# A state-space scan and a gated feed-forward net on one core: the first chunk taken as two pairs of units by time, and the first four f tiles as half products

## The chip, the cores and the metric
The kernel runs on one core of one Trainium2 chip. A core has a matrix engine (TensorE, PE in the profile), VectorE (DVE), ScalarE (ACT), GpSimd (POOL), and SyncE (SP), on whose queue all DMAs of this kernel are issued. The metric is the device time of one execution in microseconds; the time before is the median of 3 runs.

## The reference
First a scan in chunks over four batches, eight heads, 768 tokens, 32 values and 16 states per head; then a gated feed-forward net over 3072 tokens of 256 values, with 1536 inner values:

```python
for c in range(nc):                       # chunks of 32 tokens
    cum = np.cumsum(la, axis=-1)          # la = log(clip(a))
    L = np.exp(cum[:, :, :, None] - cum[:, :, None, :]) * causal
    CB = np.einsum('bhin,bhjn->bhij', Cc, Bc)
    y_intra = np.einsum('bhij,bhjd->bhid', CB * L, xc)
    y_inter = np.einsum('bhin,bhnd->bhid', Cc, state) * decay_to_i[:, :, :, None]
    y[:, :, sl] = y_intra + y_inter
    state = decay_full[:, :, None, None] * state + np.sum(Bx, axis=2)
...
x = attn_out.transpose(0, 2, 1, 3).reshape(B * S, H * D)
gate = 1.0 / (1.0 + np.exp(-(x @ w_gate)))
return (gate * (x @ w_val)) @ w_out
```

## The kernel before, in words
The kernel takes 128 tokens as a chunk (`L`), in two halves of 64 (`L2`), so there are six chunks. A **unit** is one batch of one chunk: u = 4c + b, written c_b. For a unit, `products` transposes B and C on TensorE (tile `pt`), ScalarE copies them out (`bct`), and `multiply` makes the products of C and B (tile `pcb`); `decays` scans the decay factors on VectorE (`ab`), and `weigh` multiplies the two (`m`). `within` makes the outputs within each half and the local states, with 64 tokens on the partitions: 32 by 64 outputs, two at a time for the two halves of the chunk. What the state adds comes after. From chunk 1 on, two units are finished together (`results`). The output of the scan for 512 tokens (128 of each batch) is the moving operand of the net, `xw` in float32 for chunk 0, and a pair of rounded parts, `xh` and `xl`, for the others.

The net goes over twelve f tiles of 128 inner values: a gate product `pg` and a value product `pv` each, a sigmoid on ScalarE, a product of the two on VectorE (`h`), and four projections per chunk (`po`). A weight is loaded once (`wr`, 0.5 MB; w0 to w11 for gates (even) and values (odd), two f tiles each; w12 to w17 for the projection), put together by `split_w` over VectorE, ScalarE, VectorE, ScalarE and GpSimd, and later split by `part_w` into two rounded parts. In chunk 0 the f tiles 0 to 5 (`thin`) use whole weights and `xw`: two products of 128 by 512 each. The others use six products each (line 770). Products of the net go through three PSUM banks, `mm`.

In the first chunk (class `FirstUnit`) each of the four units is one batch with both halves, done one after another. `result` makes the two halves in two PSUM tiles, `py` and `mm`; the local state of the first half is spread by a mask to a 128 by 256 tile `wide` (line 614), and two products with full 128 by 128 stationary tiles (line 620) add what that state gives the second half. f tile 0 starts with 256 tokens of the first two batches (line 750), before the other two are done.

The order on every engine is written out ahead by a planner: tasks have a due time (`DUES` where given, else one worked out from constants such as `P0`, `CONV`, `UNIT1`), and `run` repeatedly takes the task that its own cost model lets start first, among those near each other the one that is due first. So all queues are in order, and an instruction that waits holds all behind it on its engine. The DMAs use eight semaphores in turn; the ninth waits for the first. The decays of chunk 1 and later come by way of DRAM: `a` is loaded (`r`), clipped, stored as `a_z` and its running products as `a_p`, and `ab` and `pp` are loaded from these.

Of the kernel before, what the change touches and what calls it, by code (L numbers as in the profile page):

```python
# [36 lines left out]
FIRST = "b0 x0 b1 x1 b2 x2 w0 b3 x3 w1 w2 w3 r w4 w5 w6 w7 w8 w9"  # L37
# [13 lines left out]
P0 = 35.5  # L51
UNIT0 = 4.5
CONV_D = 6.3
CONV = -30.0
UNIT1 = 52.0
UNIT1_D = 7.0
FFN1 = 77.0
# [11 lines left out]
def tile_ssd_then_gated_ffn(  # L69
# [28 lines left out]
    NPLAIN = 6  # L98
    NWHOLE = 12
# [21 lines left out]
    warm_sb = hp.tile([P, P], F32, tag="h6", name="warm_sb")  # L121
# [18 lines left out]
    eye2 = hp.tile([P, L2], F32, tag="h7", name="eye2")  # L140
# [16 lines left out]
    of_row = hp.tile([NB * H, P], F32, tag="h4", name="of_row")  # L157
# [170 lines left out]
    def part_w(i):  # L328
# [3 lines left out]
        if n > 1 and plain[order[n - 2]]:  # L332
            needs.append(("used", order[n - 2]) if order[n - 2] < NF else ("proj", 0))
# [26 lines left out]
    class Unit:  # L360
# [7 lines left out]
        def products(self):  # L368

            c, b, u = self.c, self.b, self.u  # L370
            needs = [("bc", u)]
            if c:
                needs += [("bct", u - 1 if c > 1 else -1), ("cb", u - 4), ("cd", u - 4)]
            needs += [("x", 0, NB - 1)] if c == 1 else []
            pool, tag, hold = (ps_y, "py", "y") if c else (ps_mm, "mm", "banks")
            yield step("pe", 0.24 if c else 0.45, needs, [("tp", u)], **{hold: 1})
            bn, cn = (got[k, c, b // 2][:, b % 2].rearrange("p h n -> p (h n)") for k in ("bn", "cn"))
            pt = pool.tile([P, 512], F32, tag=tag, name=f"pt{self.nm}")
            nc.tensor.transpose(pt[:, :L], bn, eye)
            nc.tensor.transpose(pt[:, L : 2 * L], cn, eye)  # L380
            yield step("act", 0.9 if c else 1.1, [], [("bct", u)], **{hold: -1})
            if c:
                self.bct = wk.tile([P, 4, L], F32, tag="bct", name=f"bct{self.nm}", bufs=4)
            else:

                if ("bct", b // 2) not in got:
                    got["bct", b // 2] = hp.tile([P, 2, 4, L], F32, tag=f"h{b // 2}", name=f"bct{self.nm}")
                self.bct = got["bct", b // 2][:, b % 2]
            if c:
# [5 lines left out]
            if c == 0:  # L395
                nc.scalar.copy(self.bct[:, 1, L2:], pt[:, L + L2 : 2 * L])
            units[u] = self
            if c == 0:
                yield step("pe", 0.47, [], [("cb", u)])
                if "pcb" not in got:  # L400
                    got["pcb"] = ps_cb.tile([P, NQ, 512], F32, tag="pcb", name="pcb0")
                multiply(got["pcb"], b, self)
# [17 lines left out]
        def decayed(self):  # L420
            c, b, u = self.c, self.b, self.u
            eng = yield step(("dve", "pool"), (0.28, 0.42), [("bc", u), ("scan", u), ("y", u - 4)], [("bdec", u)], port=True)
# [40 lines left out]
    def multiply_after(*us):  # L463

        then = [u + 2 for u in us]
        yield step("pe", 0.8, [("bct", u) for u in then], [("cb", u) for u in then], cb=1)
# [97 lines left out]
    class FirstUnit(Unit):  # L564


        def spread(self):

            b, u = self.b, self.u
            yield step("pe", 1.0, [("a0",)], banks=1)  # L570
            pa = ps_mm.tile([P, 512], F32, tag="mm", name=f"pa{b}")
            for i in range(2):
                rows = slice(32 * i, 32 * i + 32)
# [11 lines left out]
        def before(self):  # L585

            u, b = self.u, self.b
            eng = yield step(("dve", "pool"), (0.2, 0.3), [("bct", u), ("p0",)], [("cd", u)], port=True)
            self.cd = wk.tile([P, L], F32, tag="cd", name=f"cd{self.nm}", bufs=4)
            engines[eng].tensor_tensor(out=self.cd[:, L2:], in0=self.bct[:, 1, L2:], in1=got["p0"][:, b], op=ALU.mult)  # L590

        def last(self, i):
            return got["p0"][:, self.b, L2 - 1 : L2]
# [4 lines left out]
        def result(self):  # L598
            u, b = self.u, self.b
            yield step("dve", 0.68, [("cb", u), ("scan", u)], [("mult", u)])  # L600
            weigh(self)
            yield step("pe", 0.75, [("xn", u), ("first", u - 1), ("bdec", u)], [("y", u)], banks=1, y=1)
            self.py = py = [
                pool.tile([P, NK + 1, L2], F32, tag=tag, name=f"{tag}{self.nm}") for pool, tag in ((ps_y, "py"), (ps_mm, "mm"))
            ]
            within(
                self, lambda i, kt, rows: py[i][rows, kt], lambda i, rows: py[i][rows, NK], lambda kt: kt == 0
            )
            yield step("dve", 0.42, [("inter", u - 2)], [("wide", u)])
            if b == 0:  # L610
                got["wide"] = hp.tile([P, NB, NQ, NG, D], F32, tag="h3", name="wide")
            wide = got["wide"][:, b]
            local = py[0][:, NK].rearrange("p (o g d) -> p o g d", o=1, g=NG)
            nc.vector.tensor_tensor(
                out=wide, in0=local.broadcast_to([P, NQ, NG, D]),
                in1=of_h.rearrange("p (q g o) -> p q g o", g=NG, o=1).broadcast_to([P, NQ, NG, D]), op=ALU.mult,
            )
            yield step("pe", 0.42, [("cd", u)], [("inter", u)])
            for kt in range(NK):
                nc.tensor.matmul(  # L620
                    py[1][:, kt], wide[:, 2 * kt : 2 * kt + 2].rearrange("p q g d -> p (q g d)"), self.cd[:, L2:],
# [388 lines left out]
```

## Time and profile before

| | |
|---|---|
| median of 3 runs | 377.67 us (376.72 to 379.18) |
| profiled execution | 376.6 us, span 374.8 us |
| TensorE busy | 364.8 us, 97% of the span |
| VectorE, ScalarE, GpSimd busy | 155.2, 151.2, 156.2 us |
| granted TensorE clock | 1.00 to 17.5 us, 0.50 to about 31 us, 1.00 to the end |
| DMA | 26.27 MB, mean 70 GB/s; in the first 60 us 100 to 390 GB/s |

An engine's busy time counts instructions, not whether the end waits for them; here TensorE's queue is nearly gapless after the first 30 us, so a change shows in the end only where it changes the length of TensorE's queue, its gaps, or its clock. In the chain and in the timelines the first column is the start from the beginning of the span and the second the duration, in us. A wait stands in brackets: the idle time ahead of the instruction, and what ended it.

### The profile page before, as it was taken

What the parts mean: (1) busy time and instruction counts of PE and PEld (TensorE: products, weight loads), DVE (VectorE), ACT (ScalarE), POOL (GpSimd) and SP (SyncE); (2) the same over time, 40 slices, a digit from 0 to 9 for tenths busy, and PEclk for the clock granted to TensorE, in tenths of its full rate; (3) what the DMA queues carried; (4) which work ended last, traced back from release to release, by engine and by line L of the source; (5) the groups of instructions that cost most, each with busy time, mean ns of one, the idle gap of its engine ahead of it and who ended that gap; (6) DMA issues with size and microseconds to landing.
All of it is one profiled execution on the core that took longest, in us unless ns stands there. A gap on an engine that the chain in (4) does not pass through costs nothing.

```text
span 374.8 us, 8050 instructions
## 1 busy us (share of the span) xinstructions
PE 364.8 (97%) x3336; PEld 285.5 (76%) x3336; DVE 155.2 (41%) x280; ACT 151.2 (40%) x319; POOL 156.2 (42%) x161
## 2 busy tenths in 40 slices
PE   8779999999899999999999999999999999999996
PEld 2356468878688888888788888788877788888885
DVE  4765576863764234253431452450142440222201
ACT  2556677333546421446511435420335420244400
POOL 4454848764768540245430155430145420145410
PEclk9958999999999999999999999999999999999999
DMA  7999975187610052414402304120000000000000
GB/s 153 137 339 168 232 246 170 33 128 144 124 31 16 0 96 63 75 39 58 83 17 58 100 0 47 27 40 28 28 3 2 2 2 28 28 2 0 0 30 28
DMA packets 89270, 26.27 MB, mean 70 GB/s; under 512 B 76306, under 2 KB 82002, under 8 KB 89234
## 3 DMA queue, kind: packets, MB, share of 16 engines
q1 hardware_dynamic: 89234, 25.76, 31.2%
q8 instruction: 26, 0.43, 0.5%
q14 instruction: 10, 0.08, 0.1%
HBM read 22.41 MB, written 3.34 MB: 69 GB/s over the span
## 4 chain that ended last, share of the span: by engine, by line
PE 90%; SPq 4%; DMA 3%; DVE 1%; issue 0%; ACT 0%; DVEq 0%
PE pg L770 25%; PE pv L770 24%; PE po L807 15%; PE po L808 7%; PE po L796 5%; PE pv L761 2%; PE pg L761 2%; PE pcb L485 2%; SPq L261 2%; PE pcb L459 2%; DMA wr<-in_moe_w_val_dram 2%; PE pcb L536 1%; SPq L268 1%; PE pcb L492 1%; SPq L295 1%; DMA ab<-a_z 1%
## 5 line engine op out<-in xcount | busy, mean ns | idle before, releaser
L731 POOL TENSOR_TENSOR h<-g,h 128x512 fp32r<-128x512 f32 x60 | 78.9, 1315 | 124.1 <-ACT h L729 121.4
L770 PE MATMUL pg<-xh,w 128*128 128x512 f32 x264 | 93.8, 396 | 0.0
L770 PE MATMUL pv<-xh,w 128*128 128x512 f32 x264 | 93.7, 396 | 0.0
L807 PE MATMUL po<-w,h 128*128 128x512 f32 x228 | 81.9, 402 | 0.0
L725 DVE TENSOR_TENSOR g<-pv,g 128x512 f32<-128x512 f32 x60 | 41.5, 691 | 91.8 <-PE pv L770 86.9
L729 ACT CAST h<-g 128x512 fp32r<-128x512 f32 x60 | 37.3, 621 | 78.4 <-DVE g L725 78.4
L808 PE MATMUL po<-w,h 128*128 128x256 f32 x228 | 63.9, 280 | 0.0
L770 PEld LDWEIGHTS pg<-xh,w 128*128 128x128 f32 x264 | 49.5, 188 | 11.4 <-issue 0.7
L770 PEld LDWEIGHTS pv<-xh,w 128*128 128x128 f32 x264 | 49.6, 188 | 10.6 <-issue 0.2
L701 ACT ACTIVATE g<-pg 128x512 f32<-128x512 f32 x72 | 43.0, 597 | 22.6 <-PE pg L770 16.4
L770 PE MATMUL pg<-xl,w 128*128 128x512 f32 x132 | 51.5, 390 | 0.0
L770 PE MATMUL pv<-xl,w 128*128 128x512 f32 x132 | 51.4, 390 | 0.0
L807 PEld LDWEIGHTS po<-w,h 128*128 128x128 f32 x228 | 42.8, 188 | 10.7 <-issue 0.2
L808 PEld LDWEIGHTS po<-w,h 128*128 128x128 f32 x228 | 43.1, 189 | 0.2
L823 ACT COPY o<-po 128x256 f32<-128x256 f32 x20 | 7.5, 373 | 67.3 <-PE po L808 66.7
L825 DVE TENSOR_TENSOR o<-po,o 128x256 f32<-128x256 f32 x20 | 8.5, 424 | 59.8 <-ACT o L823 59.8
L339 POOL TENSOR_TENSOR w<-wr,w 128x512 fp32r<-128x512 f32 x18 | 24.4, 1359 | 12.3 <-ACT w L337 9.9
L770 PEld LDWEIGHTS pv<-xl,w 128*128 128x128 f32 x132 | 24.8, 188 | 4.7
L414 DVE TENSOR_TENSOR_SCAN ab<-ab,delta 128x512 f32<-128x512 f32 x20 | 25.7, 1286 | 6.5 <-DMA ab<-a_z 6.5
L770 PEld LDWEIGHTS pg<-xl,w 128*128 128x128 f32 x132 | 24.8, 188 | 4.6
L322 POOL TENSOR_TENSOR wr<-wr 128x512 int32<-128x512 int32 x18 | 21.6, 1206 | 9.0 <-ACT wr L320 4.5
L796 PE MATMUL po<-wr,h 128*128 128x256 f32 x96 | 23.6, 393 | 0.0
(104 smaller groups left out, 380.2 us busy)
## 6 DMA issues: line engine op xcount, KB each, us to landing
ab<-a_z SPq DMA_DIRECT2D x40, 128.0 KB
wr<-in_moe_w_gate_dram SPq DMA_DIRECT2D x6, 512.0 KB
wr<-in_moe_w_val_dram SPq DMA_DIRECT2D x6, 512.0 KB
wr<-in_moe_w_out_dram SPq DMA_DIRECT2D x6, 512.0 KB
out_dram<-o SPq DMA_DIRECT2D x24, 128.0 KB
xn<-in_x_dram SPq DMA_DIRECT2D x10, 256.0 KB
bn<-in_B_dram SPq DMA_DIRECT2D x10, 128.0 KB
cn<-in_C_dram SPq DMA_DIRECT2D x10, 128.0 KB
```

What stands on the lines that cost most here:

```text
L322: nc.gpsimd.tensor_tensor(out=lw.bitcast(I32), in0=hw.bitcast(I32), in1=lw.bitcast(I32), op=ALU.add)
L339: engines[eng].tensor_tensor(out=lo, in0=lw, in1=hi.bitcast(F32), op=ALU.subtract)
L414: nc.vector.tensor_tensor_scan(out=t.rearrange("p h l -> p (h l)"), data0=t.rearrange("p h l -> p (h l)"), data1=delta.rearrange("p h l -> ...
L701: nc.scalar.activation(gs[k, f], pm, AF.Sigmoid)
L725: nc.vector.tensor_tensor(out=g, in0=pm, in1=g, op=ALU.mult)
L729: copies[eng](hh, g)
L731: engines[eng].tensor_tensor(out=hl, in0=g, in1=hh.bitcast(F32), op=ALU.subtract)
L761: nc.tensor.matmul(pm, whole[f // 2 * 2 + j][:, kt, fs], xw[0][:, kt], start=(kt == 0), stop=(kt == NK - 1))
L770: nc.tensor.matmul(pm, w[:, part, kt, fs], xx[:, kt], start=(i == 0), stop=(i == 3 * NK - 1))
L796: nc.tensor.matmul(acc[:, :DM], hs[k, f][:, js], whole[NF + f // 2][:, f % 2], start=start, stop=stop, skip_group_check=True,)
L807: nc.tensor.matmul(acc, hh, w.rearrange("p i m -> p (i m)"), start=start, stop=False, skip_group_check=True)
L808: nc.tensor.matmul(acc[:, :DM], hl, w[:, 0, :], start=False, stop=stop, skip_group_check=True)
```

## The change
A unit of the first chunk is now one half of the chunk (64 tokens) of two batches: on partitions 0 to 63 a batch of the first two, on 64 to 127 one of the other two. Units 0 and 1 are the first 64 tokens of all four batches, units 2 and 3 the last 64 (`late`). Each pair of units is finished together in one `pcb` tile. The state that goes from the first pair to the second is passed by 16 products with 32 by 64 stationary tiles (line 624); `wide` and its two full products per unit are gone. There are again twelve loads of B, C and x for the chunk, each of 64 tokens and two batches, where it was 128 tokens and one batch.

The f tiles 0 to 3 of chunk 0 are made as half products: gate and value for the 256 tokens of the first pair (index `_0`), and later for those of the second (`_1`). Each half has a PSUM bank, a sigmoid and a product of its own. The table of due times and six constants are new, so that the order of much else moves too.

On TensorE, at the start of the net, these rows stood (pg0_0 is the gate product of chunk 0's f tile 0, pv the value product; line 620 is a state product of unit 3):

```order
L750 MATMUL pg0_0_450<-xw0_256,wr0_131 128x256 x2
L620 MATMUL mm0_3_420<-cd0_3_396,wide_244 128x64 x2
L750 MATMUL pv0_0_466<-xw0_256,wr1_166 128x256 x2
L750 MATMUL pg0_0_450<-xw0_256,wr0_131 128x256 x2
L750 MATMUL pv0_0_466<-xw0_256,wr1_166 128x256 x2
L761 MATMUL pg0_1_495<-xw0_256,wr0_131 128x512 x2
```

Now there stand, at the same place (the number behind the f tile is the half; line 464 makes C times B, 490 and 497 are the products within a pair of units, 624 the state's):

```order
L714 MATMUL pg0_0_0_319<-xw0_308,wr0_134 128x256 x2
L464 MATMUL pcb0_2_330<-bct0_2_236 64x128 x16
L714 MATMUL pv0_0_0_351<-xw0_308,wr1_124 128x256 x2
L714 MATMUL pg0_1_0_357<-xw0_308,wr0_134 128x256 x2
L714 MATMUL pv0_1_0_368<-xw0_308,wr1_124 128x256 x2
L490 MATMUL pcb0_2_330<-m0_2_354,xn0_1_222 32x64 x16
L497 MATMUL pcb0_2_330<-xn0_1_222,bd0_2_227 32x64 x8
L490 MATMUL pcb0_2_330<-m0_3_364,xn0_1_222 32x64 x16
L497 MATMUL pcb0_2_330<-xn0_1_222,bd0_3_234 32x64 x8
L624 MATMUL pcb0_2_330<-cd0_2_313,m00_0_310 64x64 x4
```

The first four half products stand ahead of the second pair of units; three more rows of line 624 and the other halves of f tiles 2 and 3 follow.

Further on, around the last f tile with whole weights, TensorE had (pt1_0 are the transposes of B and C of unit 1_0):

```order
L761 MATMUL pg0_4_565<-xw0_256,wr4_279 128x512 x2
L761 MATMUL pv0_4_579<-xw0_256,wr5_263 128x512 x2
L761 MATMUL pg0_5_589<-xw0_256,wr4_279 128x512 x2
L761 MATMUL pv0_5_595<-xw0_256,wr5_263 128x512 x2
L379 MATMUL pt1_0_606<-eye_88,bn1_0_510 128x128
L380 MATMUL pt1_0_606<-eye_88,cn1_0_512 128x128
L770 MATMUL pg0_6_609<-xh0_413,w6_540 128x512
```

and has now:

```order
L804 MATMUL pg0_4_577<-xw0_308,wr4_160 128x512 x2
L804 MATMUL pv0_4_585<-xw0_308,wr5_176 128x512 x2
L386 MATMUL pt1_0_597<-eye_88,bn1_0_457 128x128
L387 MATMUL pt1_0_597<-eye_88,cn1_0_459 128x128
L804 MATMUL pg0_5_601<-xw0_308,wr4_160 128x512 x2
L386 MATMUL pt1_1_613<-eye_88,bn1_0_457 128x128
L387 MATMUL pt1_1_613<-eye_88,cn1_0_459 128x128
L804 MATMUL pv0_5_617<-xw0_308,wr5_176 128x512 x2
L464 MATMUL pcb1_1_628<-bct1_0_606 64x128 x8
L464 MATMUL pcb1_1_628<-bct1_1_621 64x128 x8
L813 MATMUL pg0_6_650<-xh0_523,w6_535 128x512
```

The transposes of units 1_0 and 1_1 and their products of C and B have moved ahead of f tile 6, the first of them ahead of f tile 5; those of unit 1_3 stand still earlier, ahead of the last half product.

On SP's queue the loads from w8 to w11 stood so (ahead of them all of the first chunk, r, nine other weights and xn1_0; bn, cn and xn are B, C and x, wr the weights):

```order
L295 DMA wr8_345<-in_moe_w_gate_dram 128x2x512
L261 DMA bn1_1_383<-in_B_dram 128x16x16
L261 DMA cn1_1_385<-in_C_dram 128x16x16
L295 DMA wr9_409<-in_moe_w_val_dram 128x2x512
L299 DMA wr17_448<-in_moe_w_out_dram 128x2x512
L268 DMA xn1_1_464<-in_x_dram 128x16x32
L299 DMA wr12_478<-in_moe_w_out_dram 128x2x512
L299 DMA wr14_490<-in_moe_w_out_dram 128x2x512
L261 DMA bn1_0_510<-in_B_dram 128x16x16
L261 DMA cn1_0_512<-in_C_dram 128x16x16
L299 DMA wr16_527<-in_moe_w_out_dram 128x2x512
L295 DMA wr11_537<-in_moe_w_val_dram 128x2x512
```

and the loads from the second pair's x to cn1_0 stand now so (ahead of them ten small loads of the first chunk, w1, w3, w0, w4, w5, w6, w2 and r):

```order
L274 DMA xn0_1_222<-in_x_dram 64x16x32 x2
L304 DMA wr7_243<-in_moe_w_val_dram 128x2x512
L304 DMA wr8_252<-in_moe_w_gate_dram 128x2x512
L269 DMA xn1_0_306<-in_x_dram 128x16x32
L262 DMA bn1_1_323<-in_B_dram 128x16x16
L262 DMA cn1_1_325<-in_C_dram 128x16x16
L304 DMA wr10_361<-in_moe_w_gate_dram 128x2x512
L304 DMA wr11_371<-in_moe_w_val_dram 128x2x512
L304 DMA wr9_378<-in_moe_w_val_dram 128x2x512
L308 DMA wr16_430<-in_moe_w_out_dram 128x2x512
L262 DMA bn1_0_457<-in_B_dram 128x16x16
L262 DMA cn1_0_459<-in_C_dram 128x16x16
```

The loads bn1_0 and cn1_0 have moved ahead of w12, w14 and xn1_1. The store of a_z, which stood behind all weights, stands ahead of w13 and w17.

The diff, cut to its core:

```diff
-    "clip": 85, "ap": 69.1, "b0": -2241.4, "x0": -1715.3, "b1": -1198.2, "x1": -353.2, "b2": -320.2, "x2": -974.3,
...
+    "ap": -250.3, "b0": -747, "c0": -1659.1, "w0": -247.3, "w1": -1093.4, "b1": -246.9, "c1": -287.9, "w2": -84.4,
...
-P0 = 35.5
+P0 = 18.0
...
+    def load_first(tag, src, late, n):
+        t = pair_of(tag, 0, 2 * late, n)
+        for i in range(2):
+            nc.sync.dma_start(
+                t[i * L2 : (i + 1) * L2].rearrange("p u h n -> p (u h) n"),
+                src[late * L2 : (late + 1) * L2, 2 * i * H : 2 * (i + 1) * H],
+            )
...
+    def first_results(*two):
+
+        late = two[0].u // 2
+        us = [t.u for t in two]
+        for t, u in zip(two, us):
+            yield step("dve", 0.70, [("cb", u), ("scan", u)], [("mult", u)])
+            weigh(t)
...
+            within(t, lambda i, kt, rows: py[rows, i, kt, 0, k], lambda i, rows: py[rows, i, 0, 1, k], lambda kt: k == 0)
+        if not late:
+            return
+        yield step("pe", 0.7, [("cd", u) for u in us] + [("first", 0)], [("inter", u) for u in us])
+        for k, t in enumerate(two):
+            for i in range(2):
+                for q in range(NQ):
+                    qs, rows = slice(32 * q, 32 * q + 32), slice(64 * (q % 2), 64 * (q % 2) + 64)
+                    nc.tensor.matmul(
+                        py[rows, i, q // 2, 0, k], got["s1", i][qs, k], t.cd[qs, i * L2 : (i + 1) * L2],
...
-            nc.vector.tensor_tensor(
-                out=wide, in0=local.broadcast_to([P, NQ, NG, D]),
...
-                nc.tensor.matmul(
-                    py[1][:, kt], wide[:, 2 * kt : 2 * kt + 2].rearrange("p q g d -> p (q g d)"), self.cd[:, L2:],
...
+    def first_outputs(late):
+
+        for i in range(2):
+            yield step("act", ACT_HALF, [("inter" if late else "y", 2 * late + 1)], [("xf", late)] if i else [])
...
+            nc.scalar.copy(out, got["py", late][:, i, :, 0])
...
+    def half_of(f, i, j):
+
+        pm = ps_mm.tile([P, 512], F32, tag="mm", name=f"p{'gv'[j]}0_{f}_{i}")
+        fs = slice(f % 2 * P, (f % 2 + 1) * P)
+        for kt in range(NK):
+            nc.tensor.matmul(
+                pm[:, : 2 * P].rearrange("p (b l) -> p b l", b=NB), whole[f // 2 * 2 + j][:, kt, fs],
+                xw[0][:, kt].rearrange("p (b s l) -> p b s l", b=NB, s=2)[:, :, i], start=(kt == 0), stop=(kt == NK - 1),
+            )
+        return pm
...
+    def half_gate(f, i):
+        before = [("pv", 0, f - 1, i)] if f else []
+        yield step("pe", GV0 / 2, [("whole", f // 2 * 2), ("xf", i)] + before, [("pg", 0, f, i)] + half_used(f, i, 0), banks=1)
+        pm = half_of(f, i, 0)
+        yield step("act", ACT_HALF, [], [("sig", 0, f, i)], banks=-1, g=1)
...
+        nc.scalar.activation(gs[0, f, i][:, : 2 * P], pm[:, : 2 * P], AF.Sigmoid)
```

More of the change, by code (lines that the diff above doesn't have):

```diff
@@ L592, in last @@
-        def last(self, i):
-            return got["p0"][:, self.b, L2 - 1 : L2]
+            engines[eng].tensor_tensor(
+                out=self.cd.rearrange("p (i l) -> p i l", i=2), in0=self.bct[:, 1].rearrange("p (i l) -> p i l", i=2),
+                in1=got["p0"].rearrange("p (i u) l -> p i u l", i=2)[:, :, u % 2], op=ALU.mult,
+            )
         def decays(self):
             yield from self.decayed()
[L598 to L614, printed above, removed]
-                out=wide, in0=local.broadcast_to([P, NQ, NG, D]),
[L616 to L620, printed above, removed]
-                    py[1][:, kt], wide[:, 2 * kt : 2 * kt + 2].rearrange("p q g d -> p (q g d)"), self.cd[:, L2:],
-                    start=False, stop=True, skip_group_check=True,
-                )
-            yield step("dve", 0.21, [("S", u - 2), ("early", u)], [("first", u)], y=-1)
-            self.s1 = state_of(u, "sm")
-            chosen(self.s1.rearrange("p (o c) -> p o c", o=1), py[0][:, NK:], 1)
-            yield step("act", 0.28, [], [("x", 0, b), ("lo", u)])
-            self.take(1)
-            yield step("dve", 0.21, [("S", u - 2)], [("after", u)], banks=-1)
-            self.after = wk.tile([P, NG * D], F32, tag="mr", name=f"mr{self.nm}")
-            chosen(self.after.rearrange("p (o c) -> p o c", o=1), py[1][:, NK:], 1)
@@ new lines, in half_value @@
+    def half_value(f, i):
+        yield step(
+            "pe", GV0 / 2, [("whole", f // 2 * 2 + 1), ("pg", 0, f, i)], [("pv", 0, f, i)] + half_used(f, i, 1), banks=1
+        )
+        pm = half_of(f, i, 1)
+        yield step("dve", DVE_HALF, [("sig", 0, f, i)], [("h", 0, f, i)], banks=-1, g=-1)
+        g = gs.pop((0, f, i))
+        if (0, f) not in hs:
+            hs[0, f] = hp.tile([P, 512], F32, tag=f"h{f}", name=f"h0_{f}")
+        by = "p (b l) -> p b l"
+        nc.vector.tensor_tensor(
+            out=hs[0, f].rearrange("p (b s l) -> p b s l", b=NB, s=2)[:, :, i], in0=pm[:, : 2 * P].rearrange(by, b=NB),
+            in1=g[:, : 2 * P].rearrange(by, b=NB), op=ALU.mult,
+        )
@@ L784, in proj @@
                 some = fs[n : n + 4]
-                needs = [("h", k, i) for i in some]
+                needs = [n for i in some for n in ([("h", k, i, 0), ("h", k, i, 1)] if halved(k, i) else [("h", k, i)])]
                 needs += sorted({("whole" if single(k, i) else "w", NF + i // 2) for i in some})
@@ L919, in tile_ssd_then_gated_ffn @@
     }
-    for b, n in ((0, 1), (1, 1), (2, 1), (3, 1)):
-        loads.update({f"{k}{b}": g for k, g in loads_of(0, b, n).items()})
+    for late in range(2):
+        for tag, src, n, needs, makes in (
+            ("b", b4, N, [], [("b0", late)]),
+            ("c", c4, N, [], [("bc", 2 * late), ("bc", 2 * late + 1)]),
+            ("x", x4, D, [], [("xn", 2 * late), ("xn", 2 * late + 1)]),
+        ):
+            loads[f"{tag}{late}"] = load(
+                2, 1.9 if tag == "x" else 1.5, needs, makes, lambda a=(f"{tag}n", src, late, n): load_first(*a)
+            )
     for i in range(NW):
@@ L952, in unit @@
             pair.append(u)
-        if u.more:
+        if u.more and c:
             task(due + STATE, f"state{u.nm}", u.state())
@@ L959, in tile_ssd_then_gated_ffn @@
         unit(UNIT0 * b, 0, b)
+    for b in range(NB):
         unit(UNIT1 + UNIT1_D * b, 1, b)
```

183 lines of the change are left out of this document (103 added, 80 removed), and 25 rows, old and new, of the table DUES.

## The prediction
> **What bounds the kernel now.** I read the page's shares and slices first, then TensorE's waits, then the clock by windows, then the chain.
>
> ```profile
> span 374.8 us, 8050 instructions
> PE 364.8 (97%) x3336; PEld 285.5 (76%) x3336; DVE 155.2 (41%) x280; ACT 151.2 (40%) x319; POOL 156.2 (42%) x161
> PE   8779999999899999999999999999999999999996
> ```
> ```profile
> PE pt L380 <- DMA cn<-in_C_dram: 1.6, 1, 1.6
> PE mm L620 <- DVE wide L614: 1.3, 2, 0.7
> PE warm L125 <- DVE warm_sb L122: 1.1, 1, 1.1
> PE pcb L459 <- DVE mr L500: 1.1, 1, 1.1
> PE py L485 <- DVE sm L500: 0.9, 1, 0.9
> ```
> ```profile
> 14.00:15.00 1.00, 0.81 (x5) 0.57 (x5) 1.00 (x2) 0.43 (x2) 0.59 (x2) 1.00 0.58 158
> 15.00:16.00 1.00, 0.07 (x1) 0.00 (x0) 1.00 (x5) 0.00 (x0) 0.11 (x1) 1.00 1.13 345
> 16.00:17.00 1.00, 0.37 (x14) 0.25 (x21) 0.21 (x1) 0.00 (x1) 0.00 (x0) 1.00 1.09 114
> 17.00:17.50 0.50, 0.50 (x48) 0.45 (x46) 0.00 (x0) 0.50 (x3) 0.00 (x0) 1.00 0.23 36
> 17.50:18.00 0.50, 0.27 (x19) 0.16 (x16) 0.00 (x0) 0.50 (x4) 0.03 (x1) 0.52 0.10 9
> 26.00:28.00 2.00, 2.00 (x6) 1.41 (x6) 1.80 (x5) 0.95 (x2) 1.09 (x1) 0.50 1.03 370
> 31.00:31.50 0.50, 0.50 (x3) 0.40 (x3) 0.50 (x2) 0.00 (x0) 0.15 (x1) 0.83 0.22 45
> ```
> TensorE is busy 97% of the span, and 60 us into it there is one wait left, the 1.1 us on "mr". So the end moves only by the first 50 us, by that wait, and by new waits. In the windows the column before the last two is the granted clock: it falls to half at 17.5, after 3.5 us with 1.75 us of work (0.81 + 0.07 + 0.37 + 0.50), and is back soon after 31.0. The chain shows where the dense work begins:
>
> ```profile
> 24.18 0.60 DVE m L473
> 25.94 2.00 PE pg L750 x4
> 27.94 0.81 PE mm L620 x4
> 28.75 1.81 PE pv L750 x4
> 30.56 1.23 PE pg L750 x4
> 31.79 0.86 PE pv L750 x4
> 32.65 1.72 PE pg L761 x4
> 48.10 1.72 PE pv L761 x4
> 50.04 1.39 PE pg L770 x6
> 55.79 0.62 PE pcb L459 x32
> 78.40 0.62 PE pcb L536 x32
> ```
> The first gate product starts at 25.94 and f tile 6 (line 770) at 50.04. That start is my marker. Between them lie f tiles 0 to 5 and one set of transposes, the 0.22 us from 49.82 to 50.04.
>
> **Part by part: the start.** A gate product now needs the first 64 tokens of all four batches, no state, and w0. Ahead of the last x load of that half the queue carries ten of the twelve small loads and three weights.
>
> ```profile
> 14.77 0.30 PE L379 MATMUL pt<-eye,bn 128*128 128x128 f32 x1 [0.20 <-DMA bn<-in_B_dram]
> 16.63 0.33 PE L380 MATMUL pt<-eye,cn 128*128 128x128 f32 x1 [1.57 <-DMA cn<-in_C_dram]
> 16.89 0.24 PE L485 MATMUL py<-m,xn 64*32 64x64 f32 x1
> 17.40 0.22 PE L492 MATMUL mm<-xn,bd 64*32 64x64 f32 x1
> 49.80 0.48 PE L770 MATMUL pg<-xh,w 128*128 128x512 f32 x1
> 96.59 0.70 PE L459 MATMUL pcb<-bct 32*64 32x128 f32 x32 [1.06 <-DVE mr L500]
> ```
> ```profile
> 18.01 0.56 DVE L309 TENSOR_SCALAR wr<-wr 128x512 f32<-128x512 f32 x1 [1.80 <-DMA wr<-in_moe_w_val_dram]
> 22.08 0.43 DVE L309 TENSOR_SCALAR wr<-wr 128x512 f32<-128x512 f32 x1 [1.77 <-DMA wr<-in_moe_w_val_dram]
> 30.35 1.09 DVE L309 TENSOR_SCALAR wr<-wr 128x512 f32<-128x512 f32 x1 [0.31 <-DMA wr<-in_moe_w_gate_dram]
> 50.80 1.22 DVE L309 TENSOR_SCALAR wr<-wr 128x512 f32<-128x512 f32 x1 [0.18 <-DMA wr<-in_moe_w_val_dram]
> 93.47 1.60 DVE L414 TENSOR_TENSOR_SCAN ab<-ab,delta 128x512 f32<-128x512 f32 x1 [3.99 <-DMA ab<-a_z]
> ```
> Before, the tenth small load (cn, behind two weights) landed at 16.63, and the third weight with all twelve behind or beside it at 18.01. Ten small and three weights lie between: 16.6, bounds 16.1 and 18.0. A unit's products within a chunk take 0.73 us (16.89 to 17.62), two units at the fallen clock some 1.9, then the two copies to xw some 0.7 (128x256 copies of 0.37 us, line 823 below). First gate product: **19.2**, bounds 18.2 (full clock) and 20.6, against 25.94.
>
> A half product takes 0.86 us at the full clock (31.79), half of the 1.72 us of a whole one, so f tiles 0 to 3 cost TensorE nothing extra. [...]
>
> The dense work before began at 25.94 and the clock came back at some 31.2, 5.3 later; so now at 24.5. From 19.2: gate half at half clock 1.9, chunk products of the second pair 1.24 (twice the 0.62 of line 459), value half 1.8, then two halves across the clock's return, some 1.9: 26.0. There stands the second pair. Its x lands after four weights, r and two small loads. A weight of 0.52 MB at 370 GB/s (window 26 to 28) takes 1.4 us. Two small loads take as much as one of the later 1.8 us loads (next part). And after the small loads the queue paused before: from 18.01 to the next weight at 22.08 are 4.1 us, 2.7 more than a weight. 16.6 + 5.6 + 1.8 + 2.3 (the pause, some of it passed under the small loads' end) = 26.3. The second pair runs there: 1.5 us, 0.3 for the 16 state tiles (half of the 32 in 0.62 us, line 536), and 0.4 for w2's split, which ends about then: f tile 2 at 28.5. The four pairs of padded state products (line 620, 0.81 us in the chain) go. VectorE's "wide" and ScalarE's copies go too, off the path.
>
> Now 12 halves, 10.3 us, a set of transposes 0.22, and f tile 4, 3.44: TensorE stands at 42.5. Each PSUM bank has half the time to be emptied, and VectorE's product with the gate for f tile 2 is queued behind the clips of w7 and w8, whose loads follow x: 0.6 us, so **43.1**. Bounds 42 and 44.5, by the start's.
>
> **The wait that comes in.** TensorE's next instruction is a transpose of chunk 1's B and C, unit 1_0, put ahead of f tile 5; all behind it on TensorE's queue waits. Before, it stood after f tile 5 and waited for nothing. When do these loads land? Before, 30.35 (w6) to 50.80 (w11) carried seven weights and six loads of chunk 1: (20.45 - 7 x 1.4) / 6 = 1.8 us each. Up to w11 the queue had carried the twelve small loads, 16 weights and these six. Up to the new cn1_0 it carries the twelve, 13 weights and five: 50.8 - 4.2 - 1.8 = **44.8**, if it pauses as long as before. With no pause after the first chunk it would be 42.5, with one more 47.1. I take 44.8, since small loads are followed by weights as often as before. Wait: 1.7 us.
>
> Marker: 44.8 + 0.22 + 1.72 + 0.22 + 1.72 + 0.62 = 49.3. By then two more sets of transposes (0.44) and chunk 1's products (0.62) are done than before, so it compares as 48.24 against 50.04: **-1.8**.
>
> **The wait on "mr".** At 96.59 TensorE waited because VectorE had been held 3.99 us at 93.47 by a scan's load. There chunk 2's products stood ahead of f tile 0 of chunk 1. Now they stand behind gate 5, and the cover for the scans is the last projection, two groups of 1.9 us. I take the 1.06 us as gone; if the scans of chunks 2 and 3 that now stand ahead of the last xl are late by over 2 us, it is back. a_z is stored earlier on SP's queue (ahead of two weights, not behind all), which speaks for it.
>
> ```profile
> L823 ACT COPY o<-po 128x256 f32<-128x256 f32 x20 | 7.5, 373 | 67.3 <-PE po L808 66.7
> L825 DVE TENSOR_TENSOR o<-po,o 128x256 f32<-128x256 f32 x20 | 8.5, 424 | 59.8 <-ACT o L823 59.8
> ```
> Eight half sigmoids and eight half products with the gate (0.37 and 0.42 us) replace four whole ones: some 0.6 us more on each engine, both 40% busy, hidden by TensorE's 0.86 us per half. Chunks 2 to 5 had no wait, and I cost their new due times at nothing; a misplaced one costs about what "mr" did, 1.1.
>
> **Sum.** -1.8 - 1.1 = -2.9 on a profiled run of 376.6 (span 374.8 and 1.8 around it): 373.7. The runs' median is 1.1 higher, 377.67, so **374.8**.
>
> **Rivals.** *Loads in time*: the queue pauses less (its pause at 18 to 22 came between loads that now have others behind them), chunk 1's B and C land by 43, and TensorE never waits: 1.7 us better, 373.1. With no pause anywhere (another us off the landing of 42.5) and the clock never fallen, TensorE stands there at 40.8 and the loads land at 41.5, so the marker compares as 44.9: -5.1, and 371.5 with the 1.1. For it: only 1.7 us part the two walks, and each has bounds of over 1. Chance 0.37.
>
> *The clock falls at the wait.* 1.7 us idle is what the 3.5 us before 17.5 held. One window of half clock costs 1.7 us, two 3.4: 376.5 to 378.2. Against it: the 1.06 us at 96.59 left the clock full, and the products then were small ones. [...] Chance 0.09.
>
> *Slower: the queue is late for chunk 1.* If the small loads of 64 partitions each bring two more pauses of 2.3 us, cn1_0 lands at 49.4, TensorE waits 6.3 instead of 1.7 (+4.6), the clock falls (+2.5), and the decays behind it on SP's queue keep the 1.1: 383. It is slower than before from a landing at 47.7, or 45.2 with the clock fallen. The trace has only one load that stopped TensorE, the cn of 1.6 us. Chance 0.13.
>
> *Weight loads not hidden*, the rule above: 24 passes at their 188 ns (line 770's PEld mean in the next row) are 4.5 us, 379.3; chance 0.02.
>
> ```profile
> L770 PEld LDWEIGHTS pg<-xh,w 128*128 128x128 f32 x264 | 49.5, 188 | 11.4 <-issue 0.7
> ```
> **Numbers.** The forecast keeps 0.39. About 1% (3.8 us) is what a measurement can tell here. Faster by over 1%, below 373.9: the first rival and a sixth of the forecast's spread (its landing some 1 us earlier), 0.42. Slower, above 381.4: 0.12, nearly all of the third. Within 1%: 0.46. The range runs from 371.5, the first rival's better end, to 379.5, and leaves out most of the third rival and some 0.05 below.
>
> **What would show it.** Right: line 714's first product near 19; the transposes of bn1_0 and cn1_0 waiting for a DMA at 43 to 45, f tile 6 near 49, no wait of "mr" near 95. Wrong: a first gate product after 21, TensorE waiting for x or for VectorE between 26 and 33, the clock at half after 30, or waits in chunks 2 to 5.

## The result, and the profile after
The changed kernel took 373.72 us (373.36 to 374.85) beside 377.69 for the one before (376.72 to 379.18): ratio 0.9906, interval 0.9878 to 0.9934. In a second set of executions it was 373.24 beside 377.03, ratio 0.9907 (0.9878 to 0.9936). So it gained 3.5 us, 0.9%; the prediction was 374.8, in a range of 371.5 to 379.5, with a wait in the middle of its argument that turned out to be small or absent.

The profiled execution took 374.85 (span 373.0), the longest of the first four; the shortest had a span of 371.5. From its page:

```profile
span 373.0 us, 8123 instructions
PE 360.9 (97%) x3376; PEld 287.0 (77%) x3376; DVE 157.0 (42%) x277; ACT 151.1 (41%) x314; POOL 150.1 (40%) x159
PE   7788999999999999999999999999999999999996
```
TensorE's waits (in total, how often, the longest):

```profile
PE pt L386 <- DMA bn<-in_B_dram: 3.1, 2, 1.6
PE pg L714 <- issue: 2.9, 2, 1.5
PE warm L126 <- DVE early L123: 1.1, 1, 1.1
PE pt L386 <- ACT bct L401: 1.0, 1, 1.0
PE pt L387 <- DMA cn<-in_C_dram: 0.6, 1, 0.6
```
The wait on "mr" is gone, as are those on "wide" and "sm". The loads of chunk 1 stop TensorE for 0.6 us. New are two waits that end with "issue", which means that the profile shows nothing that ended them: 1.44 us ahead of the first gate product, which ScalarE's copy of xw explains (it ended at 21.08), and 1.50, called a stand below. The chain, at the start of the net, at the gate product of f tile 5, at f tile 6 (line 813 now) and at chunk 1's first gate product:

```profile
21.18 2.05 PE pg L714 x4
...
46.31 1.73 PE pg L804 x4
...
50.60 1.59 PE pg L813 x6
...
94.57 1.38 PE pg L813 x6
```
The net starts at 21.18 instead of 25.94. But f tile 6 starts at 50.60, later than before (50.04). By then 1.06 us more of chunk 1's work is done, so it compares as 49.54, 0.5 ahead. With the 1.06 of "mr" that makes 1.6 of the 1.8 us by which the spans differ; 0.2 is unexplained. TensorE's timeline shows what came between:

```profile
17.51 0.47 PE L386 MATMUL pt<-eye,bn 128*128 128x128 f32 x1 [0.99 <-ACT bct L401]
...
31.04 0.59 PE L714 MATMUL pg<-xw,wr 128*128 128x256 f32 x2
33.12 0.71 PE L714 MATMUL pg<-xw,wr 128*128 128x256 f32 x2 [1.50 <-issue]
...
45.98 0.33 PE L387 MATMUL pt<-eye,cn 128*128 128x128 f32 x1 [0.61 <-DMA cn<-in_C_dram]
```
The second and third rows are one group, the four passes of pg_3_0's two products. Between the two products TensorE stood for 1.50 us, where the program has no wait at all.

### The profile page after: what moved, and what is told of

Same layout as the page of the kernel before. It is cut to its first block, busy times and chain, and to the rows that moved or that the text cites. A ratio compares the mean times of both kernels' runs of the same rounds, so it can differ in the third digit from the quotient of the medians.

```text
span 373.0 us, 8123 instructions
## 1 busy us (share of the span) xinstructions
PE 360.9 (97%) x3376; PEld 287.0 (77%) x3376; DVE 157.0 (42%) x277; ACT 151.1 (41%) x314; POOL 150.1 (40%) x159
## 4 chain that ended last, share of the span: by engine, by line
PE 88%; SPq 5%; DMA 4%; POOL 1%; issue 1%; DVE 0%; ACT 0%
PE pv L813 25%; PE pg L813 24%; PE po L850 15%; PE po L851 7%; PE po L839 6%; DMA cn<-in_C_dram 2%; SPq L304 2%; PE pcb L464 2%; PE pcb L490 2%; PE pcb L541 2%; SPq L262 1%; DMA bn<-in_B_dram 1%; SPq L274 1%; PE pcb L497 1%; POOL wr L331 1%; PE pt L386 1%
## 5 line engine op out<-in xcount | busy, mean ns | idle before, releaser
L779 ACT CAST h<-g 128x512 fp32r<-128x512 f32 x59 | 36.6, 621 | 75.7 <-DVE g L775 75.7
L754 ACT ACTIVATE g<-pg 128x512 f32<-128x512 f32 x68 | 40.7, 599 | 14.7 <-PE pg L813 13.8
L419 DVE TENSOR_TENSOR_SCAN ab<-ab,delta 128x512 f32<-128x512 f32 x20 | 28.0, 1406 | 8.3 <-DMA ab<-a_z 8.2
L331 POOL TENSOR_TENSOR wr<-wr 128x512 int32<-128x512 int32 x18 | 19.6, 1091 | 20.0 <-ACT wr L329 17.9
```

The costliest lines, as they stand in the source:

```text
L331: nc.gpsimd.tensor_tensor(out=lw.bitcast(I32), in0=hw.bitcast(I32), in1=lw.bitcast(I32), op=ALU.add)
L419: nc.vector.tensor_tensor_scan(out=t.rearrange("p h l -> p (h l)"), data0=t.rearrange("p h l -> p (h l)"), data1=delta.rearrange("p h l -> ...
L754: nc.scalar.activation(gs[k, f], pm, AF.Sigmoid)
L779: copies[eng](hh, g)
```

## Experiments
All experiments take over the changed kernel's order of every queue, entry by entry, and move or add only what their diff shows. Theories: **L**, the loads of chunk 1's B and C set when f tile 6 starts (the prediction's); **Q**, TensorE's own queue sets it. The first two runs are to decide between them.

**The same kernel again, and the transposes later.** Edit of the second, on TensorE (pcb are the products of both units; ScalarE's copies move with the transposes):

```diff
- pt1_0  pg0_5  pt1_1  pv0_5  pcb1_0,1_1  pg0_6  pt1_2  pv0_6  pg0_7
+ pg0_5  pv0_5  pt1_0  pg0_6  pt1_1  pv0_6  pg0_7  pt1_2  pcb1_0,1_1
```


> The changed kernel once more, nothing altered: 373.7 again, give or take 0.6, and a second profile of it. The first one was its longest execution (374.85, span 373.0 against 371.5 of its shortest). If the 1.5 us in which TensorE stood between the two products of pg_3_0 (31.6 to 33.1, released by nothing that the profile shows) belongs to the program, it is here again at the same two instructions; if it is chance, it is not, TensorE reaches the transposes of unit 1_0 some 1.5 us sooner than 45.1, at 43.6, and waits 2.1 us there instead of 0.6 if the load of cn1_0 sets the pace (theory L), or f tile 6 starts 1.5 us sooner, at 49.1, if TensorE's own queue sets it (theory Q).

> The transposes of unit 1_0 stand behind f tile 5 instead of ahead of it, those of 1_1 and the products of both a place further down; all else in the order stays. Theory L (the load of cn1_0 sets when f tile 6 starts): the wait is gone, and the time falls by its length, 0.6 us if TensorE comes as late as in the first profile, up to 2.1 if it comes at 43.6: 373.1 to 371.6. Theory Q (TensorE's own queue sets it, the wait is by chance): 0 to 0.6, 373.7 to 373.1. Rival W: f tile 6 comes too early for its weight's or x's second part, or the value product for that of w7; a new wait there takes the gain, 373.7.

Measured: 373.24 (372.30 to 374.48) and 373.60 (372.99 to 373.84). First the chain of the same kernel's second profile (span 371.5), then its timeline:

```profile
21.76 2.04 PE pg L714 x4
...
49.12 1.59 PE pg L813 x6
```
```profile
32.10 1.03 PE L714 MATMUL pg<-xw,wr 128*128 128x256 f32 x4
...
44.44 0.27 PE L386 MATMUL pt<-eye,bn 128*128 128x128 f32 x1
44.55 0.27 PE L387 MATMUL pt<-eye,cn 128*128 128x128 f32 x1
```
The net starts 0.58 later than in the first profile, yet f tile 6 comes 1.48 sooner: no stand in pg_3_0 (its four passes are one row at 32.10), and no wait at the transposes, though TensorE reaches them at 44.44, sooner than 45.10. So the landing varies too, by over 1.4 us. The sum 0.58 - 1.50 - 0.61 = -1.53 accounts for the 1.48. With the transposes later (its timeline) the stand was back, at the same two passes:

```profile
30.55 0.59 PE L714 MATMUL pg<-xw,wr 128*128 128x256 f32 x2
32.94 0.71 PE L714 MATMUL pg<-xw,wr 128*128 128x256 f32 x2 [1.80 <-issue]
```
There the wait for cn1_0 is gone from the profile, no other has come at f tile 6 (rival W), and the time is no better. The times alone can't tell 0.6 us (the interval of each is 1.1 us to either side). But in the second profile f tile 6 came without any wait for a load: theory L falls, the wait is 0 to 0.6 us and not the limit.

**Keeping the clock up.** Products on zeros that nobody reads:

```diff
+ def filler(n): n products of 128 by 256 into an unused tile
  # ahead of the transposes of units 0_0, 0_1, 0_2
+ filler(3)
  # behind the first pair's products
+ filler(2)
```


> Eleven products of 128 by 256 on zeros (0.43 us each at the full clock, no reader) fill TensorE's idle time between 7 and 21 us: three ahead of the transposes of each of units 0_0, 0_1 and 0_2, two behind the first pair's products. The order is otherwise the changed kernel's. If they keep the clock at 1.00, the first pair's products, the first gate product, the 32 products of line 464 and the value product take 1.3, 0.9, 0.6 and 0.9 us instead of 1.6, 2.05, 1.1 and 1.5. By theory Q the start of f tile 6 and the end move by that sum, some 2 us: 371.7. By theory L nothing beyond the wait of 0.6 to 2.1 can be won, less what the fillers cost: 373.1 to 373.7, with a longer wait at the transposes of 1_0. Rival G: w2 is put together at 28.7 only, so f tile 2 starts at 28.8 whatever the clock, and all is won back by 0.4 us at most: 373.3 to 373.7, with a wait for GpSimd ahead of f tile 2.

> Both edits at once. Theory L: the two add up to more than either alone, since the wait no longer takes what the clock gives: 1 to 2 us beyond the later transposes alone, 372.1 to 370. Theory Q: the fillers' 2 us and nothing more, 371.7. Rival G (w2 sets f tile 2): no more than 0.4 beyond the later transposes alone.

376.13 (0.9972, 0.9941 to 1.0002) and 376.08 (0.9984, 0.9962 to 1.0007), where both theories expected a gain or no change: nearly the whole gain is lost, though the mean granted clock rose from 0.98 to 0.995. TensorE's timeline, of the fillers alone and then with the later transposes:

```profile
26.10 0.92 PE L714 MATMUL pv<-xw,wr 128*128 128x256 f32 x3 [2.07 <-issue]
...
31.57 0.45 PE L624 MATMUL pcb<-cd,m 32*64 32x64 f32 x12 [1.20 <-issue]
```
```profile
27.93 0.56 PE L624 MATMUL pcb<-cd,m 32*64 32x64 f32 x20
32.56 0.45 PE L624 MATMUL pcb<-cd,m 32*64 32x64 f32 x12 [4.07 <-issue]
```
The stand has moved to two other places, the same two in both kernels, again with no wait in the program. Rival G (w2 sets f tile 2) did not decide: w2 was together at 30.0, itself held up by a sigmoid behind the first stand, and f tile 2 began at 31.95, right behind the second. Without its two stands of 3.27 us TensorE would have been there at 28.7, 0.5 before the changed kernel's 29.20: the clock's gain, and small.

That gives a third theory, **F**. A record is a weight load and a matmul. Counted from the start of the program, the stand in pg_3_0 lies behind 346 records; the eleven fillers add 22 (18 of them ahead of the first pair's products), and the new stands lie behind 219 and 346 again, 127 records or 254 instructions apart. The count leaves out the semaphore instructions of the same program, so a place can come out a record or two off. The page's queues, whole execution and then a window of 0.2 us at 30.4 of the changed kernel's first profile, show transfers of instructions (packets, MB, share of 16 engines), 0.43 MB in 26 of them, some 16.5 KB each:

```profile
q8 instruction: 26, 0.43, 0.5%
```
```profile
q8 instruction: 1, 0.02, 38.5%
```
TensorE's 2 x 3376 instructions in 26 transfers are 260 each, an estimate that takes all 26 as TensorE's, since the row names no engine. So by theory F TensorE takes its program in blocks of some 128 records, and stands where the next block isn't there yet.

**Moving the borders.** 42 small products on zeros ahead of the first pair, 84 records; a control with 128, one whole block; and 84 made in part of large ones.

```diff
  # ahead of the transposes of units 0_0, 0_1, 0_2:
+ filler(0, 22)  -           filler(0, 20)   # 84 records, alone and with the later transposes
+ filler(3, 10)  filler(3, 10)  filler(1, 14)   # large, small; one large behind the first pair
+ filler(0, 26)  filler(0, 12)  filler(0, 26)   # 128 records
```


> 42 products of 32 by 64 on zeros (84 records, each a weight load and a matmul) stand in TensorE's idle time, 22 ahead of the transposes of unit 0_0 and 20 ahead of those of 0_2; all else as in the changed kernel. Theory F: TensorE takes its instructions in blocks of 16 KB, 256 of them, that is 128 records, and asks for the next block when it enters one; a block of small products lasts 4 us, its successor comes 3.9 to 8.3 us after the entry, and TensorE stands for the difference. In the changed kernel the borders lie at the 10th record of the second pair's products (27.6) and between the two products of pg_3_0 (33.1). With 84 records more they lie in the middle of the first pair's products, in the middle of the second pair's, and at f tile 4; no block lasts under 9 us, and the stand between 28 and 34 is gone in this profile. The time then falls by what the load of cn1_0 lets through: 372.3 to 373.2. Rival R (the stand is in the products' own waits or chance): it stays between 31 and 33 in some profile, at pg_3_0, and the time is 373.4 as before.

> The 84 records and the transposes of unit 1_0 behind f tile 5. Theory F: neither the stand of 1.8 us nor the wait of 0.6 to 2.1 us; 373.6 (with the late transposes alone, whose profile had the stand) less 1.8: 371.8, up to 0.3 more if other runs stood for less. Rival R: 373.6.

> As the one before, but the 84 records are made of 8 products of 128 by 256 (three ahead of unit 0_0's transposes, three ahead of 0_1's, one ahead of 0_2's, one behind the first pair) and 34 small ones, so that the clock may stay at 1.00 as it did with eleven large ones. Theory F with the clock: the fillers alone lost 2.9 us (376.1 against 373.2) because the borders lay at pv_0_0 and within the state's products, where TensorE stood 2.1 and 1.2, or 1.5 and 4.1 us; with the borders elsewhere the full clock gives its 1 to 2 us: 370 to 371.5. Rival G: w2 is put together at 28.7 and holds f tile 2, so the clock gives 0.4 us at most: 371.4 to 371.8. Rival D: the full clock and more work ahead make the loads or VectorE late in some other way, as much as before: 375 or more.

> The control: 64 small products on zeros, 128 records, one whole block, so that the borders lie at the same instructions as in the changed kernel. Theory F: the stand may come again, between the two products of pg_3_0 and nowhere else near, and the time is that of the changed kernel, 373 to 374. Rival R' (the small products help by something else, a warmer clock or a later start): no stand, and as fast as with 84 records.

375.67, 375.77, 376.93 (ratios 0.9979, 0.9978 and 1.0001, each interval holding 1) and 380.34 (1.0083, 1.0054 to 1.0112), where 370 to 374 was expected. The times missed because the fillers were dear; in the third the clock fell all the same, at 12.5. All small ones wrote the same place, and one after the other took 112 ns a record at half clock. From the timeline with 84 records, a profile of one of its longer executions (379.26; six of the ten took 375.2 to 375.8, four 378.2 to 379.3):

```profile
17.21 4.47 PE L202 MATMUL unused<-early 32*64 32x64 f32 x40
...
27.09 2.05 PE L714 MATMUL pg<-xw,wr 128*128 128x256 f32 x4 [1.44 <-issue]
```
The net started at 27.09, 5.9 late (1.44 is the wait for ScalarE's copy of xw). f tile 6 followed at 55.11, 4.5 later than 50.60: 5.9, and 1.2 of slower clock up to the second pair, less the stand of 1.5 and the wait of 0.6, would be 5.0. So a late start goes through to f tile 6, which is theory Q. The borders between blocks behaved as F has it: no stand in the three profiles with 84 records, and in the control it is back in pg_3_0, behind 474 records now, with 0.28 us (1.31 instead of 1.03):

```profile
38.38 1.31 PE L714 MATMUL pg<-xw,wr 128*128 128x256 f32 x4
```

**Cheap borders, no early halves, and both best edits.** 32 small products that turn over four banks and row groups (20 to 27 ns a record); the four half products ahead of the second pair moved behind it:

```diff
  # behind units 0_0 and 0_1's products of line 464
+ filler(pcb, 32)
```
```diff
- pg0_0_0  pcb0_2,0_3  pv0_0_0  pg0_1_0  pv0_1_0  (second pair)  pg0_2_0
+ pcb0_2,0_3  (second pair)  pg0_0_0  pv0_0_0  pg0_1_0  pv0_1_0  pg0_2_0
```


> The borders of the instruction blocks moved again, now by products that pass quickly: 32 products of 32 by 64 on zeros (64 records), turn by turn on the four row groups and into the four banks of pcb, behind the first two units' products of line 464, where TensorE stood 1.2 to 1.6 us (14.3 to 15.9) in the changed kernel. At the 17 to 34 ns a record that products of this kind took, they are over by 15.4 to 16.4, so the first gate product starts at 21 to 22 as before, unlike with the 84 records that started it at 24 to 27. Theory F (TensorE stands for its next block of 256 instructions): no stand between 28 and 34; 0.3 to 1.0 us off the 373.3 of the changed kernel's nine executions, more of it where they stood longest: 372.3 to 373.0, the longest under 374. Rival R (the stand at pg_3_0 has another cause): it is there in this profile or the time is 373.3 or more.

> The four half products that stand ahead of the second pair of units (gate and value of f tiles 0 and 1 for the first 256 tokens, with their sigmoids and products) moved behind it; all else as in the changed kernel, so that the net starts only when all 512 tokens of the chunk are there. Theory Q (TensorE's queue sets f tile 6): the second pair starts at 26 instead of 27.5, f tile 0 at 28 instead of 21.2, 16 halves instead of 12 follow, four of them at half clock, and f tile 6 starts 2 to 2.8 us later: 375.3 to 376.1, between the changed kernel and the one before. Theory L (the loads of chunk 1 set it): 0.6 us later at most, 373.3 to 373.9.

> The 64 records and the transposes of unit 1_0 behind f tile 5, the candidate for a faster version. Theory F: the late transposes alone took away the wait for cn1_0, but in their profile TensorE stood 1.8 us for a block; without it 371.8 to 372.8. Rival R: 373.6 as with the late transposes alone.

64 records: 374.53 (373.26 to 376.49; ratio 0.9920, 0.9890 to 0.9950), not the gain that was expected. In its profile, of the longest execution, there was no stand between 28 and 34, but one of 2.34 us earlier, in the middle of the first pair's last products, which delayed the net to 25.19:

```profile
20.51 0.47 PE L497 MATMUL pcb<-xn,bd 64*32 64x64 f32 x10
23.33 0.42 PE L497 MATMUL pcb<-xn,bd 64*32 64x64 f32 x4 [2.34 <-issue]
```
The borders had moved out of the way of the second pair and into the first: the second row begins behind 220 records of the program. With the later transposes as well, 373.92 (372.26 to 376.12; ratio 0.9904, 0.9867 to 0.9940): no stand in its profile, the shortest span of all profiles, 370.7, but executions up to 376. Behind the place of the stand another wait appeared:

```profile
33.03 1.14 PE L714 MATMUL pg<-xw,wr 128*128 128x256 f32 x4 [0.83 <-DVE h L738]
```
It is pg_0_1, whose bank VectorE must empty first. In the changed kernel's first profile that product of VectorE ran from 33.17 to 33.58. Without the stand pg_0_1 would have been due at 32.8 and would have waited till about 33.6; it started at 34.53. So of the delay of 1.7 us some 0.9 are net. That is worked out, not measured.

Without the early halves: 376.62 (0.9983, 0.9961 to 1.0004). Its longest wait on TensorE (at 25.46, ahead of the second pair, where the early halves stood) and its chain:

```profile
PE pcb L490 <- DVE m L478: 3.4, 1, 3.4
```
```profile
28.41 2.00 PE pg L714 x4
...
52.16 1.59 PE pg L813 x6
```
f tile 6 is 1.6 to 3.0 us behind the changed kernel's two profiles, the time by the ratios (0.9983 less 0.9907) 2.9 us longer. Theory Q again. The early halves are most of the gain: without them no difference from the kernel before can be told. What the new state products and the other due times give by themselves was not tried.

**What holds the block up.** On top of the later transposes, the loads of B and C of units 1_2 and 1_3 (bn1_1 and cn1_1, 4096 small packets beside the stand, not 8192 as the expectation has it) stand behind four weights, and the transposes of unit 1_3 behind f tile 8's gate product:

```diff
- SyncE: bn1_1  cn1_1  w10  w11  w9  w16  bn1_0  cn1_0
+ SyncE: w10  w11  w9  w16  bn1_1  cn1_1  bn1_0  cn1_0
```


> As the late transposes (unit 1_0's behind f tile 5), and the loads of B and C of units 1_2 and 1_3, 8192 packets that ran from 26 to 33 us, behind the weights w10, w11, w9 and w16 that followed them; the transposes of unit 1_3 go behind f tile 8's gate product with them. TensorE's instructions up to the second border (pg_3_0) are the changed kernel's. Theory F1 (the many small packets of B and C hold up the block of instructions): its packet starts at most 1.2 us after TensorE enters the block before it, at 27 to 28.6, instead of the 2.9 and 3.1 us of the two profiles in which TensorE stood, and TensorE does not stand at pg_3_0: 371.8 to 372.8. Theory F2 (any load in the queue does, weights as well): it starts 2 us or more after, TensorE stands there again, 373.6 as with the late transposes alone, or more. In the one profile of the changed kernel without a stand the packet started 0.5 us after, with the same loads, so one profile alone decides between the two only together with the time.

373.76 (373.16 to 374.13; ratio 0.9913, 0.9884 to 0.9941), with a stand of 0.28 us at the same place:

```profile
32.76 0.71 PE L714 MATMUL pg<-xw,wr 128*128 128x256 f32 x2 [0.28 <-issue]
```
The packet of instructions still started some 2 us after TensorE entered the block before, so F2, weights as well as small packets, fits better; one profile doesn't settle it. All stands, with the changed kernel's second profile and the control, in us (entered: TensorE starts the block before, by the count of records; packet: its start, within 0.2; needed: TensorE has done all that it has):

| kernel | entered | packet | needed | resumed | stand |
|---|---|---|---|---|---|
| changed, first profile | 27.5 | 30.4 | 31.6 | 33.1 | 1.50 |
| changed, second | 28.6 | 29.0 | 32.5 | | 0 |
| later transposes | 27.1 | 30.0 | 31.1 | 32.9 | 1.80 |
| fillers, first stand | 19.3 | 23.0 | 24.0 | 26.1 | 2.07 |
| fillers, second stand | 26.1 | 28.8 | 30.4 | 31.6 | 1.20 |
| fillers, later transposes, first stand | 18.1 | 21.4 | 22.8 | 24.2 | 1.45 |
| fillers, later transposes, second stand | 24.2 | 29.2 | 28.5 | 32.6 | 4.07 |
| control, 128 records | 34.9 | 36.6 | 39.0 | 39.0 | 0 (row 0.28 longer) |
| 64 records | 16.4 | 20.6 | 21.0 | 23.3 | 2.34 |
| B and C behind weights | 28.4 | 30.4 | 32.5 | 32.8 | 0.28 |

TensorE goes on 2.4 to 3.4 us after the packet's start wherever it stood, and in these rows the packet starts 0.4 to 5 us after the entry. Later it can start before: the fourth packet of the changed kernel's first profile started at 57.0, and TensorE reached record 474, its entry by the same count, at 58.7. So what asks for a block is not the entry as it is counted here. None of these edits beat the changed kernel (nine executions, 372.30 to 374.85, median 373.36).

## Why the prediction was right, and where it was not
- **First gate product at 19.2**: 21.18 and 21.76, outside the bounds of 18.2 to 20.6. TensorE waited for no load at the first pair's products; the step left out three places in the queues. The second pair's transposes stand ahead of these products, and the second of them waits 0.99 us for ScalarE to empty the one buffer (17.51, above). VectorE makes m for the second unit only at 17.30, behind a part of a weight (line 325), and in the second profile at 17.98; there TensorE waited 0.96 us for it. So the products began at 18.12 and 18.71 instead of 16.6, and with m ready only at 17.98 the transposes alone don't explain it. And ScalarE's second copy to xw stood 0.56 behind VectorE's mask product on its way. VectorE's m and ScalarE's copy in the first profile, and the products in the second:

```profile
17.30 0.68 DVE L478 TENSOR_TENSOR m<-pcb,ab 128x512 f32<-128x512 f32 x1
```
```profile
20.71 0.37 ACT L636 COPY xw<-pcb 128x256 f32<-128x256 f32 x1 [0.56 <-DVE m L505]
```
```profile
18.71 0.68 PE L490 MATMUL pcb<-m,xn 64*32 64x64 f32 x32 [0.96 <-DVE m L478]
```
- **Half products cost nothing extra**: right. They follow each other every 0.86 to 0.87 us. The rival of weight loads not hidden is out: no run shows the rule that it names, nor its 4.5 us.
- **Clock back at 24.5**: 25.1 and 26.7 in the two profiles, 3.9 and 4.9 behind the start instead of 5.3. It fell 6 to 8 us sooner than before, at 11.5 and 9.6, which the prediction did not see.
- **Second pair and f tile 2 (26.3, 28.5)**: 27.45 and 29.20, in the second profile 28.51 and 30.26. TensorE came late and waited for neither x nor w2. The 0.6 us for VectorE's product with the gate show as a wait in neither profile; with 64 records and later transposes such a wait took 0.83 (33.03, above).
- **The wait that comes in, 1.7 us**: this is the step that failed. TensorE arrived at 45.10 and 44.44 instead of 43.1, and the loads landed at 45.9 and before 44.4 instead of 44.8: 0.6 and 0. The estimate of the landing was fair; TensorE was 1.3 to 2 us later than thought, by the late start and the stand. So that the forecast came out near the right time was in part luck: TensorE's lateness took the place of the wait.
- **Marker -1.8**: -0.5 in the first profile, -2.0 in the second (49.12 less 1.06 against 50.04). **The wait on "mr", -1.1**: right, gone in both profiles. **Sum -2.9**: -1.8 and -3.3 by span, -4.0 and -3.8 by the medians.
- **Rivals.** Of "loads in time" the second profile has the condition, no wait, and nearly the time, but by a late TensorE rather than early loads. The queue late for chunk 1 never happened. The clock did not fall at a wait in the changed kernel, neither behind the stand of 1.50 us nor behind the wait of 0.61 (granted 1.00 from 25.5 on in the first profile). It fell behind the stand of 4.07 us, below, and stayed at half for some 3.4 us; half of that is 1.7, what the rival reckons for one window, where the third rival has 2.5 for a fallen clock. Of what was named as a sign of being wrong, the first gate product after 21 came; the time stayed in the range because the wait for chunk 1's loads shrank by 1.1 and 1.7 us.

## What to carry to other kernels
To start a dense stage on the part of its input that is ready can win most of the time by which TensorE otherwise stands, if its queue is full from there on: here 2.9 us, beside a wait of 3.4 without it. A wait that is argued into a gap has to be checked against the lateness of everything ahead of it. Where TensorE stands with no releaser among many small products and heavy loads, as here for 0.3 to 4.1 us, count the records, and see whether the stand keeps its count when the program is shifted: here it came behind 219 or 220, 346 or 474 records, and theory F, that TensorE lacks instructions there, rests on that.

## What the runs showed of the hardware
**Instruction blocks.** In the first 40 us, with the loads running, TensorE stood 0.3 to 4.1 us at places behind 219 or 220, 346 or 474 records of the program, with 0, 22, 64 or 128 records put in ahead of them; not every execution stood there, and with 84 none of the three profiles shows a stand. The places lie 126 to 128 records apart; the transfers carry some 16.5 KB each (0.43 MB in 26) and, if all of them are TensorE's, 260 of its instructions. That they are blocks of its program is theory F. What asks for the packet was not seen, only its start; that the loads delay it is argued from where the stands occur.

**The clock.** It fell at 11.5 after 3.5 us in which TensorE was busy for 2.59, with products of 32 rows and few transposes (the column before the last two is the granted clock):

```profile
8.00:11.50 3.50, 2.59 (x28) 1.40 (x28) 3.29 (x6) 2.28 (x6) 1.77 (x3) 0.99 0.96 188
11.50:12.00 0.50, 0.50 (x3) 0.26 (x4) 0.50 (x1) 0.00 (x0) 0.33 (x1) 0.50 0.27 98
25.00:25.50 0.50, 0.50 (x4) 0.45 (x3) 0.21 (x2) 0.00 (x0) 0.32 (x1) 0.88 0.21 29
```
With fillers of 84 records, part of them large, it fell at 12.5, though TensorE was busy for nearly all of the 3.5 us before:

```profile
9.00:12.50 3.50, 3.44 (x43) 2.22 (x42) 2.51 (x5) 1.94 (x6) 0.97 (x2) 1.00 1.00 232
12.50:13.00 0.50, 0.50 (x2) 0.41 (x2) 0.50 (x1) 0.26 (x1) 0.50 (x1) 0.50 1.13 319
```
So the busy time of the profile alone does not tell when the clock falls. It also fell after the stand of 4.07 us (fillers and later transposes) and was at half for some 3.4 us (0.08, 3.00 and 0.34, worked out from the last three rows):

```profile
28.50:32.50 4.00, 0.00 (x0) 0.00 (x0) 0.00 (x0) 0.00 (x0) 0.00 (x0) 1.00 0.87 92
32.50:33.00 0.50, 0.43 (x13) 0.37 (x12) 0.00 (x0) 0.00 (x0) 0.00 (x0) 0.92 1.45 136
33.00:36.00 3.00, 3.00 (x8) 2.46 (x8) 2.70 (x10) 2.23 (x6) 0.00 (x0) 0.50 0.97 237
36.00:37.00 1.00, 1.00 (x5) 0.85 (x4) 0.30 (x1) 1.00 (x3) 0.92 (x1) 0.83 1.05 391
```
The stands of 1.5 and 1.8 us left it at full: behind the first it was 1.00 from 33 to 36, and behind the second two passes took 0.71 us as they did behind the first, with the same mean clock of 0.982 (behind the stand of 4.07, four passes took 2.07). How long a stand has to be for the clock to fall was not shown.
